# VectorE's first addition placed ahead of the first eviction in attentions 3 to 8, and a new order of PE, VectorE and ScalarE in the second attention

## The chip, the cores and the metric

One core of one Trainium2 chip. The metric is the device time of one execution in microseconds (us); the number given for a kernel is the median of several executions. The engines are TensorE (PE, with its weight loads as PEld), VectorE (DVE), ScalarE (ACT), GpSimd (POOL) and SyncE (SP), which here only issues DMAs. Each engine works through its own list of instructions in the order of the program.

## What is computed

A normalised attention for 8 batches and 12 heads, then a two-layer MLP with a tanh GELU over its output:

```python
batch, n_heads, seq, head_dim = (8, 12, 448, 64)
n_tokens, d_model, d_ff = (3584, 768, 2048)

q_n, k_n = (rmsnorm(q, g_q), rmsnorm(k, g_k))
scores = scale * np.matmul(q_n, k_n.transpose(0, 1, 3, 2))
scores = scores - np.max(scores, axis=-1, keepdims=True)
attn = np.exp(scores)
attn = attn / (np.sum(attn, axis=-1, keepdims=True) + 1e-09)
return np.matmul(attn, v).astype(np.float32)
...
h = x @ w_in
g = 0.5 * h * (1.0 + np.tanh(c * (h + 0.044715 * h * h * h)))
return (g @ w_out).astype(np.float32)
```

Inputs and output are float32; the kernel multiplies in bfloat16 and accumulates in float32.

## The kernel before

The kernel goes through the batches b = 0 to 7. Each has an attention and a first MLP layer of its own (`mm1_pair`, L516: 96 matmuls with `win`, then GELU on ScalarE). The second MLP layer of a batch (matmuls with `wout`) is spread through the attention of the next batch, so that PE has work while ScalarE computes the exponentials. The first attention (`first_attention`, L679) has another order; attentions 2 to 8 (b = 1 to 7) run in `attention` (L552), and the change touches only the two tables that it reads: `SECOND` (L545) for b = 1 and `STEADY` (L539) for b = 2 to 7, which are attentions 3 to 8.

Heads are taken four at a time: c = 0, 1, 2. For each c there are NT = 7 units t of 64 keys, so an attention has 21 units, u0 to u20. A table has three parts.

The first part is the order of PE, a string of words:

- `u`, a unit (L327): 4 matmuls give the scores of 64 keys into a two-bank PSUM buffer; ScalarE's `exp` (L341) turns it into `ex[:, t]`. Two `u` in one word follow each other directly.
- `r`, a round of the second MLP layer of the batch before (L487): 4 matmuls of 64x64 weights. 32 rounds fill one output tile in PSUM ("full"); an attention has 3 tiles, 96 rounds. `12r` is twelve rounds. In the middle of each tile, after 16 rounds, PE waits for its own last matmul (`follows`, L466).
- `s`, the sums of the exponentials for the next c (L385, weights `ones`).
- `x`, the products with V for the next c (L385, weights `vb`).

The second part is the order of VectorE:

- `A`, `B`, `F`, `G` with the number c (L353, L356, L358, L360): they add up the seven `ex[:, t]` of c, so that `s` needs fewer matmuls. `A` adds units 0, 1 and 2, 3; `B` adds 4, 5 to it; `F` folds the two halves together; `G` adds the seventh unit. For c = 2 there is no `G`. In attention 2 there is none of them for c = 1, and `s1` has 28 matmuls.
- `T`, `R`, `S`, `M` with c: transpose the sums out of PSUM (L395), reciprocal (L400), spread (L407), and `M` multiplies the product with V by it into `xT` (L420), which feeds the first MLP layer. `M` reads the PSUM buffer of `x`, `T` that of `s`.
- `E0`: evict output tile 0 from PSUM into `osb` (L505), whose stores SP issues.
- In attention 2 only: `L0`, `L1` set one element each in the buffers of raw q and k (L142), so that the loads behind them start then; `K0` is a gain on `kT` (L323), behind which GpSimd is held (L764) until it squares q and k of batch 2 (L164); `a0` to `a5` reduce these squares (L173).

The third part says before which exponential ScalarE evicts which tile: `{14: 1, 21: 2}` is tile 1 before the exponential of u14, and tile 2 after the last. In `SECOND` all three tiles are evicted by ScalarE (L511, two copies each).

The two lists are merged into one program at every word of PE: an entry of VectorE or ScalarE is put down as soon as it is at the head of its list and what it needs has been put down (`needs`, L579). This decides the order on each engine, not the times; at run time semaphores make each instruction wait for its inputs.

PSUM has four two-bank buffers in `rounds` (L66, L968). A unit, `s` or `x` takes the one that was taken longest ago (`pair`, L70):

```python
def pair(name):
    rounds.append(rounds.pop(0))
    return rounds[-1]
```

An output tile takes one out of this ring (`quartered`, L473) and puts it back at the end when it is full, so that while a tile is being filled three buffers go round. Who takes a buffer waits for the last reader of what was in it: the exponential of a unit, `T`, `M`, or the eviction of a tile.

Of the kernel before, what the change touches and what calls it, by code (L numbers as in the profile page):

```python
# [17 lines left out]
def kernel(  # L18
# [497 lines left out]
    def mm1_pair(i, cs=range(HP), b=0, js=range(2)):  # L516
# [22 lines left out]
    STEADY = (  # L539
# [4 lines left out]
    )  # L544
    SECOND = (  # L545
# [4 lines left out]
    )  # L550

    def attention(b, side, extra, ends):  # L552
# [448 lines left out]
```

## Time and profile before

| | before |
|---|---|
| median of 3 runs | 399.84 us (399.36 to 400.06) |
| the profiled execution | 400.39 us |
| its span in the profile | 398.3 us |
| granted TensorE clock | 1.00 |
| TensorE matmuls busy | 384.8 us (97%) |
| ScalarE busy | 281.6 us (71%) |
| VectorE busy | 231.5 us (58%) |
| GpSimd busy | 123.6 us (31%) |

The span is what lies between the first and the last instruction that the profile shows; the execution's own time is 2.1 us longer. In a timeline row stand the start, the duration (of all instructions merged into the row), the engine, the line of the kernel, the operation, output and input, the count, and in brackets how long the engine had been idle before it and what ended that. In the view of waits a row names who waited for whom, the sum in us, how often, and the longest. Attention 2 lies between 50.8 and 78.5 us of the span, attention 3 between 96.8 and 124.6 us, and each later one begins some 46.1 us after the one before.

### The profile page before, as it was taken

What the parts mean: (1) busy time and instruction counts of PE and PEld (TensorE: products, weight loads), DVE (VectorE), ACT (ScalarE), POOL (GpSimd) and SP (SyncE); (2) the same over time, 40 slices, a digit from 0 to 9 for tenths busy, and PEclk for the clock granted to TensorE, in tenths of its full rate; (3) what the DMA queues carried; (4) which work ended last, traced back from release to release, by engine and by line L of the source; (5) the groups of instructions that cost most, each with busy time, mean ns of one, the idle gap of its engine ahead of it and who ended that gap; (6) DMA issues with size and microseconds to landing.
All of it is one profiled execution on the core that took longest, in us unless ns stands there. A gap on an engine that the chain in (4) does not pass through costs nothing.

```text
span 398.3 us, 12138 instructions
## 1 busy us (share of the span) xinstructions
PE 384.8 (97%) x5359; PEld 231.9 (58%) x5359; DVE 231.5 (58%) x358; ACT 281.6 (71%) x361; POOL 123.6 (31%) x104
## 2 busy tenths in 40 slices
PE   8799998999999999999999999999999999999996
PEld 3365576755665566655765556655666556655564
DVE  5998837976596339925488246943499204870010
ACT  6995499777994789847995689947897359934301
POOL 4994506294008140273105440091303600000000
PEclk9999999999999999999999999999999999999999
DMA  8999999989514991359712994159622611120033
GB/s 281 306 223 207 200 187 311 195 198 254 108 44 74 268 202 46 81 135 277 135 44 51 208 238 94 43 97 267 90 53 71 131 30 41 43 63 2 0 79 81
DMA packets 66553, 54.34 MB, mean 136 GB/s; under 512 B 37572, under 2 KB 62276, under 8 KB 66500
## 3 DMA queue, kind: packets, MB, share of 16 engines
q1 hardware_dynamic: 54144, 41.48, 41.5%
q0 software_dynamic: 12128, 11.80, 19.2%
q8 instruction: 42, 0.69, 0.7%
q10 hardware_dynamic: 228, 0.28, 0.2%
q14 instruction: 11, 0.09, 0.1%
HBM read 45.61 MB, written 11.01 MB: 142 GB/s over the span
## 4 chain that ended last, share of the span: by engine, by line
PE 82%; DVE 7%; ACT 6%; DMA 2%; POOL 1%; issue 1%; SPq 0%; DVEq 0%
PE t L524 36%; PE t L487 22%; PE t L461 9%; PE t L385 9%; ACT ex L341 5%; PE t L333 5%; DVE es L356 2%; DMA rawq<-in_q_dram 2%; DVE es L353 2%; DVE osb L505 1%; DVE es L358 1%; DVE es L360 1%; POOL g L164 1%; PE h L434 1%; PE tp L294 0%
## 5 line engine op out<-in xcount | busy, mean ns | idle before, releaser
L341 ACT ACTIVATE ex<-t,shift 128x896 bf16<-128x896 f32 x168 | 155.0, 1012 | 8.0 <-PE t L333 7.0
L524 PE MATMUL t<-xT,win 128*128 128x448 bf16 x756 | 144.8, 352 | 0.0
L487 PE MATMUL t<-wout,g 64*64 64x384 bf16 x2688 | 134.7, 323 | 1.4 <-DVE xT L420 1.2
L524 PEld LDWEIGHTS <-win 128*128 128x128 bf16 x756 | 73.8, 98 | 68.9 <-issue 0.7
L531 ACT ACTIVATE g<-t 128x896 bf16<-128x896 f32 (+1 forms) x70 | 58.1, 842 | 64.6 <-PE t L524 64.6
L487 PEld LDWEIGHTS <-g 64*64 64x64 bf16 x2688 | 79.4, 107 | 36.1 <-issue 4.1
L173 DVE TENSOR_REDUCE ss<-sq 128x14 f32<-128x896 f32 (+3 forms) x45 | 44.6, 997 | 56.2 <-ACT sq L162 51.8
L333 PE MATMUL t<-qT,kT 64*64 64x448 bf16 x672 | 57.7, 351 | 2.4 <-ACT lg L198 0.9
L276 POOL TENSOR_TENSOR nrmq<-rawq,rinv 128x896 bf16<-128x896 f32 (+1 forms) x21 | 34.7, 1652 | 13.7 <-DVE o L239 6.4
L461 PE MATMUL t<-wout,g 128*128 128x384 bf16 (+1 forms) x240 | 37.6, 316 | 0.0
L764 POOL COPY mark<-es 1x1 bf16<-1x1 bf16 x6 | 1.1, 177 | 116.0 <-DVE es L358 116.0
L276 POOL TENSOR_TENSOR nrmk<-rawk,rinv 128x896 bf16<-128x896 f32 x20 | 33.6, 1679 | 0.0
L385 PE MATMUL t<-ex,vb 64*64 64x448 bf16 x588 | 31.4, 349 | 0.0
L461 PEld LDWEIGHTS <-g 128*128 128x128 bf16 x240 | 22.5, 98 | 15.0 <-issue 2.1
L395 DVE STREAM_TRANSPOSE st<-t 128x448 f32<-128x448 f32 x42 | 24.6, 623 | 9.2 <-PE t L385 9.2
L333 PEld LDWEIGHTS <-kT 64*64 64x64 bf16 x672 | 21.8, 106 | 13.0 <-DVE kT L303 2.9
L385 PEld LDWEIGHTS <-vb 64*64 64x64 bf16 x672 | 20.9, 107 | 10.8 <-issue 0.8
L407 DVE STREAM_TRANSPOSE rb<-rc 128x896 f32<-128x896 f32 (+1 forms) x25 | 26.7, 1067 | 0.3
L505 DVE COPY osb<-t 128x768 f32<-128x768 f32 x6 | 5.7, 957 | 35.9 <-PE t L487 23.2
L164 POOL TENSOR_TENSOR sq<-rawq 128x896 f32<-128x896 f32 (+1 forms) x9 | 13.6, 1511 | 36.8 <-DVE ss L173 32.7
L353 DVE TENSOR_TENSOR es<-ex 128x1792 bf16<-128x1792 bf16 x20 | 21.1, 1054 | 4.4 <-ACT ex L341 4.4
L420 DVE TENSOR_TENSOR xT<-t,rb 128x896 bf16<-128x896 f32 x21 | 22.6, 1076 | 0.9
(99 smaller groups left out, 272.5 us busy)
## 6 DMA issues: line engine op xcount, KB each, us to landing
rawq<-in_q_dram SPq DMA_DIRECT2D x23, 448.0 KB, 4.4
rawk<-in_k_dram SPq DMA_DIRECT2D x23, 448.0 KB, 5.2
out_dram<-osb SPq DMA_DIRECT2D x42, 192.0 KB, 2.7
vb<-in_v_dram POOLq DMA_DIRECT2D x6, 672.0 KB, 7.4
win<-in_moe_w_in_dram POOLq DMA_DIRECT2D x8, 384.0 KB, 10.5
wout<-in_moe_w_out_dram POOLq DMA_DIRECT2D x2, 1536.0 KB, 22.3
out_dram<-osb SPq DMA_DIRECT2D x26, 96.0 KB, 2.3
vb<-in_v_dram POOLq DMA_DIRECT2D x2, 448.0 KB, 17.8
```

What stands on the lines that cost most here:

```text
L173: nc.vector.reduce_sum(sss[b][:, seat(b, c), "qk".index(n), hs, ts], squares(b, c, n, hs, ts), axis=AX.X)
L276: eng.tensor_mul(nrms[n, b, c][:, ts].rearrange("p t a d -> p a t d"), raws[n, b, c][:, :, ts], root[:, :, ts].to_broadcast([P, 2, m, D]),)
L333: nc.tensor.matmul(sc[r * R:(r + 1) * R, a, :S], kT[rs, c, t, r], qT[b][rs, c, :, r], start=True, stop=True,)
L341: nc.scalar.activation(exs[b, c][:, t], scs.pop((b, c, t))[:, :, :S], AF.Exp, scale=scale, bias=shift)
L353: nc.vector.tensor_add(es, ex[:, :2], ex[:, 2:4])
L385: nc.tensor.matmul(o[r][a * D:(a + 1) * D], vb[b % 2][rs, 2 * c + a, i] if what else ones[rs], es[i][rs, a], start=(i == 0), stop=(i == n ...
L395: nc.vector.transpose(st[:, r].rearrange("p a b -> p (a b)"), o[r])
L407: nc.vector.transpose(oas["rb"][:, rs].rearrange("p r s -> p (r s)"), rc.to_broadcast([128, (rs.stop - rs.start) * m, 32]),)
L461: nc.tensor.matmul(o, g[:, f, i * 128:(i + 1) * 128], wout[:, f, lo:hi], start=(f == 0), stop=(f == nf - 1),)
L487: mm = nc.tensor.matmul(o[a * R:(a + 1) * R, bank, :HD], g[rs, f, at:at + R], wout[rs, f, half * HD:(half + 1) * HD], start=(turn == 0 and ...
L524: nc.tensor.matmul(h[:, j, :S], win[:, c, f * 128:(f + 1) * 128], xT[b][:, c], start=(c == 0), stop=(c == HP - 1),)
L531: nc.scalar.activation(g[:, 2 * i + ks.start:2 * i + ks.stop, (b % 2) * S:(b % 2 + 1) * S], h[:, ks, :S], AF.Gelu_apprx_tanh)
```

## The change

Two tables are replaced. In `STEADY` only the first two entries of VectorE's list change places. In `SECOND` all three parts are new.

```diff
     STEADY = (
         "2r u 2r u 12r uu 11r u 3r u 2r 3r u 4r u 4r u 5r uu 3r s 4r u 4r u 3r u 2r x 1r u 4r u 5r"
         " uu 6r su 5r u 9r u 2r xsx",
-        "E0 A0 B0 F0 G0 T0 R0 A1 S0 B1 M0 F1 G1 T1 A2 R1 B2 F2 S1 T2 M1 R2 S2 M2",
+        "A0 E0 B0 F0 G0 T0 R0 A1 S0 B1 M0 F1 G1 T1 A2 R1 B2 F2 S1 T2 M1 R2 S2 M2",
         {14: 1, 21: 2},
     )
     SECOND = (
-        "2r u 3r u 4r u 7r 1r u 7r u 3r u 5r uu 13r u 3r us 4r u 4r uu 7r u 1r xusu 2r u 7r u 1r u"
-        " 6r uu 7r x 6r s 3r x",
-        "A0 L0 B0 F0 G0 L1 T0 R0 K0 S0 a0 a1 M0 a2 T1 a3 R1 a4 S1 A2 a5 B2 F2 M1 T2 R2 S2 M2",
-        {7: 0, 14: 1, 21: 2},
+        "3r u 5r uu 8r u 7r uu 9r u 5r u 4r u 7r us 4r u 4r u 3r uu 4r x 1r usu 3r u 6r u 2r u 5r"
+        " uu 10r x 6r sx",
+        "A0 L0 B0 F0 G0 L1 T0 R0 K0 S0 a0 M0 a1 T1 a2 R1 a3 S1 A2 a4 B2 a5 F2 M1 T2 R2 S2 M2",
+        {6: 0, 14: 1, 21: 2},
     )
```

The amount of work is the same in both kernels. The lists of GpSimd and SP have the same instructions in the same order. In `SECOND` the first eviction stands before the exponential of u6 instead of u7; `M0` and `T1` each stand behind one reduction fewer (`a0` and `a1` are ahead of `M0` before, `a0` alone after), and the reductions that are left over follow later, the last between `B2` and `F2`; and with the new order of PE the ring deals out its buffers differently: before, output tile 2 takes the buffer of `x0` (which `M0` reads), after it is u15 that takes this buffer.

## The prediction

> **What bounds the kernel now.** I read the busy shares and the chain that ended last first, then the waits, then the timelines of attentions 2 and 3.
>
> ```profile
> PE 384.8 (97%) x5359; PEld 231.9 (58%) x5359; DVE 231.5 (58%) x358; ACT 281.6 (71%) x361; POOL 123.6 (31%) x104
> ...
> PE 82%; DVE 7%; ACT 6%; DMA 2%; POOL 1%; issue 1%; SPq 0%; DVEq 0%
> ```
>
> PE sets the time. The other engines enter the chain only where PE stands, so the change is worth the PE stalls that it removes or makes. The waits name them:
>
> ```profile
> ACT ex L341 <- PE t L333: 7.0, 14, 0.9
> PEld L385 <- DVE es L360: 6.0, 6, 1.0
> PE t L385 <- DVE es L360: 3.7, 6, 0.7
> PE t L487 <- DVE xT L420: 1.2, 1, 1.2
> ```
>
> Six times, once in each of attentions 3 to 8, PE waits for `G0` (L360) before `s0`. Once output tile 2 (L487) waits for `M0` (L420), in attention 2. And ScalarE waits 14 times for a unit of PE: the two engines run close together.
>
> Attention 3, in its timeline:
>
> ```profile
> 98.72 10.01 ACT L341 ACTIVATE ex<-t,shift 128x896 bf16<-128x896 f32 x11
> 103.34 0.96 DVE L505 COPY osb<-t 128x768 f32<-128x768 f32 x1 [4.62 <-PE t L487]
> 104.21 1.08 DVE L353 TENSOR_TENSOR es<-ex 128x1792 bf16<-128x1792 bf16 x1
> 105.28 0.36 PE L333 MATMUL t<-qT,kT 64*64 64x448 bf16 x4
> 105.40 1.09 DVE L356 TENSOR_TENSOR es<-es,ex 128x1792 bf16<-128x1792 bf16 x1
> 106.52 0.62 DVE L358 TENSOR_TENSOR es<-es 128x896 bf16<-128x896 bf16 x1
> 106.66 0.66 PE L487 MATMUL t<-wout,g 64*64 64x384 bf16 x12
> 107.25 0.62 DVE L360 TENSOR_TENSOR es<-es,ex 128x896 bf16<-128x896 bf16 x1
> 107.93 0.38 PE L385 MATMUL t<-es,ones 64*64 64x448 bf16 x4 [0.61 <-DVE es L360]
> 108.14 0.82 PE L487 MATMUL t<-wout,g 64*64 64x384 bf16 x16
> 108.79 0.36 PE L333 MATMUL t<-qT,kT 64*64 64x448 bf16 x4
> 108.98 0.82 PE L487 MATMUL t<-wout,g 64*64 64x384 bf16 x16
> 109.21 2.80 ACT L341 ACTIVATE ex<-t,shift 128x896 bf16<-128x896 f32 x3 [0.47 <-PE t L333]
> 111.89 0.81 ACT L505 COPY osb<-t 128x768 f32<-128x768 f32 x1
> 112.78 5.50 ACT L341 ACTIVATE ex<-t,shift 128x896 bf16<-128x896 f32 x6
> 115.69 0.36 PE L333 MATMUL t<-qT,kT 64*64 64x448 bf16 x4
> 118.31 1.09 DVE L356 TENSOR_TENSOR es<-es,ex 128x1792 bf16<-128x1792 bf16 x1
> 118.76 1.01 ACT L341 ACTIVATE ex<-t,shift 128x896 bf16<-128x896 f32 x1 [0.48 <-PE t L333]
> ```
>
> VectorE stands idle for 4.62 us until tile 0 is full, then runs E0, A0, B0, F0, G0 without a break until 107.87. Eleven exponentials take 10.01 us, one every 0.90 us and each about 1.01 long, so the fourth (u3), the last that A0 needs, ends near 98.72 + 3 x 0.90 + 1.01 = 102.43. A0 could have run in the idle time and was held by E0. A round of four L487 matmuls goes by in 0.163 us (the 16 at 108.14 until the unit at 108.79), so the three rounds from 106.66 are issued by 107.15, and `s0` stands from 107.15 to 107.93: 0.78 us, of which the profile, which counts to the modelled end of a matmul, shows 0.61.
>
> **Part 1, STEADY: A0 ahead of E0.** PE, POOL, SP and ACT keep their order; only two entries of VectorE change places. A0 starts at some 102.5, and E0 behind it at about 103.5, 0.1 to 0.2 later than before. Who waits for E0: u8, which takes tile 0's buffer (counting the ring), at 105.28. E0 ends near 104.5, so 0.8 us cover it. Tile 0's store issues with it, and nothing on PE waits for that. B0 follows at about 104.4 instead of 105.40 (its inputs u4 and u5 end at 104.23 by the same count), F0 and G0 each 1.0 earlier, and G0 is done near 106.9. PE asks for it at 107.15. The stall of 0.78 us is gone.
>
> The row for the order on VectorE is A0 at 104.21, 1.8 us after its inputs were there. The Trainium skill's page "TensorE: Matmul & The Clock Gate", section "Architectural detail: the array is 16× 32×32, not 1× 128×128", says that the scalar and vector engines keep strictly to the order of their queues. The trace agrees: A0 waited behind E0 until 103.34 + 0.87. By that rule E0 in its turn cannot pass an A0 that comes late, which is the slower rival below; without the rule the eviction would start at 103.34 as before, and the sum would be the same.
>
> What is late next is ScalarE. With PE 0.78 us ahead, u11 (108.79) is written by 108.01, its scores are there at 108.37, and ScalarE goes straight on from 108.73. So ScalarE gains only the 0.48 us from 108.73 to 109.21, and then works without a break through the eviction at 111.89 and the six exponentials from 112.78. u18 at 115.69 takes the buffer of u16, whose exponential is the third of these six: it ends at 112.78 + 2 x 0.90 + 1.01 = 115.59. That leaves 0.1 us in hand before; after, that exponential ends 0.48 earlier and u18 can't come 0.78 earlier, only some 0.5. Likewise B2 (118.31) starts when u19's exponential ends (118.28), so F2 and `s2` gain 0.5. ScalarE's second wait, 0.48 at 118.76, stays. Behind the attention come PE's own matmuls, which shift with it.
>
> I take 0.50 us for each attention, nearest to ScalarE's 0.47 of idle time. From above the bound is PE's stall, 0.78. From below I take 0.30: the chain F0, G0 or the eviction may slip by 0.1 to 0.2 where buffers come free with under 0.1 us in hand (u12, u14 and u18 by my count). Six times: 3.0 us, from 1.8 to 4.7.
>
> **Part 2, SECOND.** Attention 2, in its timeline:
>
> ```profile
> 52.38 6.61 ACT L341 ACTIVATE ex<-t,shift 128x896 bf16<-128x896 f32 x7
> 59.59 6.58 ACT L341 ACTIVATE ex<-t,shift 128x896 bf16<-128x896 f32 x7
> 59.97 0.62 DVE L360 TENSOR_TENSOR es<-es,ex 128x896 bf16<-128x896 bf16 x1
> 61.11 0.39 PE L385 MATMUL t<-es,ones 64*64 64x448 bf16 x4
> 64.66 1.52 PE L385 MATMUL t<-ex,vb 64*64 64x448 bf16 x28
> 65.33 1.09 DVE L173 TENSOR_REDUCE ss<-sq 128x14 f32<-128x896 f32 x1 [0.88 <-POOL sq L164]
> 66.03 0.89 ACT L511 COPY osb<-t 128x384 f32<-128x384 f32 x2
> 66.23 1.52 PE L385 MATMUL t<-ex,ones 64*64 64x448 bf16 x28
> 66.97 1.08 DVE L173 TENSOR_REDUCE ss<-sq 128x14 f32<-128x896 f32 x1 [0.55 <-POOL sq L164]
> 67.55 0.39 PE L333 MATMUL t<-qT,kT 64*64 64x448 bf16 x4
> 67.98 1.08 DVE L420 TENSOR_TENSOR xT<-t,rb 128x896 bf16<-128x896 f32 x1
> 69.11 0.52 PE L487 MATMUL t<-wout,g 64*64 64x384 bf16 x8 [1.18 <-DVE xT L420]
> 69.52 0.64 DVE L395 STREAM_TRANSPOSE st<-t 128x448 f32<-128x448 f32 x1
> 75.49 0.63 DVE L358 TENSOR_TENSOR es<-es 128x896 bf16<-128x896 bf16 x1
> 76.17 0.38 PE L385 MATMUL t<-es,ones 64*64 64x448 bf16 x4
> 78.49 2.82 PE L524 MATMUL t<-xT,win 128*128 128x448 bf16 x14
> ```
>
> From 52.38 to 66.03 ScalarE has fourteen exponentials and an eviction without a break, and PE, with three buffers in the ring, can't get ahead of it: until `s1` (66.23) a new order of PE gains nothing that lasts. Moving the first eviction by one exponential leaves this sum as it is. I keep u15 at 67.55.
>
> The stall behind it goes. PE was done with u15 at 67.55 + 0.19 = 67.74 (a unit goes by in 0.19: from 108.79 to the rounds at 108.98) and then stood for tile 2's buffer until M0 (67.98 + 1.08) at 69.11: 1.37 us. After, M0 stands behind a0 alone: it starts at 65.33 + 1.09 = 66.42 at the latest and ends by 67.50. Its waiter is now u15, due at 67.55, and behind it on PE everything. With `s0` ready at 60.59 + 0.06 instead of 61.11 (the old order puts it behind a unit and rounds; the new one reaches it at about 60.65), T0, R0, K0 and the squares on POOL come up to 0.46 earlier, and M0 as soon as x0 ends, so 0.05 to 0.5 us are in hand. Tile 2 now takes tile 1's buffer, free after the eviction (66.03 + 0.89 = 66.92).
>
> From 69.11 to 78.49 PE had 9.38 us of work; after has the same rounds, units, `x1`, `s2`, `x2` in another order. T1 starts behind M0 and a1 at about 68.0 (before 69.52), F2 5.97 us later before, now up to 0.6 more for one more reduction ahead of it: it ends by 68.0 + 5.97 + 0.6 + 0.63 = 75.2, and PE asks for `s2` at 67.74 + 7.49 (32 rounds of 0.163, five units of 0.19, `x1` of 1.32 like the 28 matmuls from 66.23 to 67.55) = 75.2. So 0 to 0.1 is lost there. I take 1.40 us. From below: if POOL's squares are no earlier, M0, a1 and T1 shift by 0.45, and F2 with them: 1.37 - 0.45 = 0.9. From above: 1.37 and some 0.2 because `s2` at 76.17 started right on F2's end (75.49 + 0.63 = 76.12) and may have waited for it: 1.6.
>
> **Sum.** 3.0 + 1.4 = 4.4 us, between 2.7 and 6.3. Against the profiled execution, 400.39 us (span 398.3 and 2.1 around it), that is 396.0. The median of the runs shown, 399.84, lies 0.55 lower, so I expect a median of 395.4.
>
> **The rivals.**
>
> 1. *PE's stall in attentions 3 to 8 only changes its name.* If u12, u14 or u18 wait for exponentials by all that `s0` gained, STEADY is worth nothing and 399.84 - 1.4 = 398.4 us results. For it: the 0.1 us in hand at u18. Against it: ScalarE's idle 0.47 us at 109.21, put down to PE, in the very place.
>
> 2. *All of the stall comes through.* If ScalarE makes up the missing 0.28 us in its second wait (0.48 at 118.76), it is 6 x 0.78 + 1.4 = 6.1: 393.7 us. Against it: u18 and B2 hang on exponentials that come earlier than that wait.
>
> 3. *Attention 2 gains nothing*, because u15 in place of tile 2 stands for M0, held by a0 and POOL: 399.84 - 3.0 = 396.8. Against it: M0 has one reduction fewer ahead of it, at least 1.0 us.
>
> 4. *Slower: E0 is late behind A0.* The eviction can't pass A0, and u8 stands for tile 0's buffer, with all of PE behind it. It decides if A0 starts after 103.3, since A0 and E0 take 1.9 together and u8 is due at 105.28. Were A0 released by the sixth exponential (98.72 + 5 x 0.90 + 1.01 = 104.23) in place of the fourth, E0 would end at 106.2, u8 stand for 0.9, and `s0` come 0.9 late: 6 x 0.9 = 5.4 lost, 1.4 won: 403.8 us. Against it: A0 waits for nothing but exponentials up to u3, and the idle row of 4.62 us shows VectorE free.
>
> 5. *Nothing is seen*, both parts being taken up by ScalarE: 399.8.
>
> **How the numbers follow.** Forecast 0.72 (2.7 to 6.3 off, less its ends); rival 1 0.09, rival 2 0.06, rival 3 0.05, rival 4 0.05, rival 5 0.03. The likeliest is 395.4. The bounds of both parts give 393.5 to 397.1; I end the range at 393.6, which takes in rival 2, and reach toward rival 1 on the other side: 393.6 to 397.9. About 0.2%, 0.8 us, is what a measurement can tell from no change. Faster: forecast and rivals 1 to 3, 0.92, less 0.02 for a rival 1 with a weak attention 2: 0.90. Same: 0.05. Slower: 0.05.
>
> **What would show it.** In the profile after: the wait of L385 for `es` L360 falls from 3.7 to under 0.5 us; A0 starts 3.8 us after the attention's first exponential, E0 about 1 us behind it; the exponential wait on PE (7.0) falls to about 4, one of two per attention being gone; attentions 3 to 8 follow each other by some 45.6 instead of 46.1 us; the wait of L487 for `xT` L420 is gone, and L524 starts at about 77.1 instead of 78.49. The forecast is wrong if PE waits at L333 for exponentials by more than 0.3 us in each attention, if u8 waits for L505, or if u15 of attention 2 waits for L420.

## The result, and the profile after

| | before | after |
|---|---|---|
| median, first comparison | 399.75 us (399.36 to 400.06, 4 runs) | 394.81 us (394.49 to 397.43, 4 runs) |
| ratio | | 0.9891, 95% interval 0.9848 to 0.9934 |
| median, two later comparisons | 400.47; 399.98 us | 394.29; 393.62 us |
| their ratios | | 0.9851 (0.9829 to 0.9873); 0.9834 (0.9815 to 0.9854) |
| profiled execution (first) | 400.39 us, span 398.3 | 394.85 us, span 392.7 |

The change is faster, by 4.9 us at first and by some 6 in the two later comparisons. The page of after shows PE with its share of the closing chain up from 82% to 92%, and VectorE's down from 7% to nothing:

```profile
PE 383.7 (98%) x5359; PEld 236.2 (60%) x5359; DVE 231.1 (59%) x358; ACT 280.0 (71%) x361; POOL 123.6 (31%) x104
...
PE 92%; ACT 4%; DMA 2%; POOL 1%; SPq 0%; issue 0%; DVE 0%
```

The view of waits of after has no row of L385 for L360 any more, and none of L487 for L420. ScalarE waits for units of PE half as often, and A0 is now what waits, for its exponentials, on a VectorE that has nothing else to do:

```profile
DVE es L353 <- ACT ex L341: 34.9, 7, 11.6
...
ACT ex L341 <- PE t L333: 3.5, 7, 0.8
```

Attention 3 in the timeline of after. Its first exponential starts at 98.04 (before 98.72), so 0.68 is to be taken off before's times to compare:

```profile
98.04 12.71 ACT L341 ACTIVATE ex<-t,shift 128x896 bf16<-128x896 f32 x14
101.78 1.09 DVE L353 TENSOR_TENSOR es<-ex 128x1792 bf16<-128x1792 bf16 x1 [3.79 <-ACT ex L341]
102.79 0.95 DVE L505 COPY osb<-t 128x768 f32<-128x768 f32 x1
103.65 1.08 DVE L356 TENSOR_TENSOR es<-es,ex 128x1792 bf16<-128x1792 bf16 x1
104.61 0.36 PE L333 MATMUL t<-qT,kT 64*64 64x448 bf16 x4
105.50 0.63 DVE L360 TENSOR_TENSOR es<-es,ex 128x896 bf16<-128x896 bf16 x1
106.47 0.36 PE L385 MATMUL t<-es,ones 64*64 64x448 bf16 x4
107.31 0.36 PE L333 MATMUL t<-qT,kT 64*64 64x448 bf16 x4
110.57 0.87 ACT L505 COPY osb<-t 128x768 f32<-128x768 f32 x1
110.83 0.36 PE L333 MATMUL t<-qT,kT 64*64 64x448 bf16 x4
111.30 5.53 ACT L341 ACTIVATE ex<-t,shift 128x896 bf16<-128x896 f32 x6
114.21 0.36 PE L333 MATMUL t<-qT,kT 64*64 64x448 bf16 x4
116.87 1.09 DVE L356 TENSOR_TENSOR es<-es,ex 128x1792 bf16<-128x1792 bf16 x1
117.28 1.01 ACT L341 ACTIVATE ex<-t,shift 128x896 bf16<-128x896 f32 x1 [0.44 <-PE t L333]
```

A0 starts 3.74 us behind the first exponential, E0 behind it 4.75 (before 4.62), and u8 finds tile 0's buffer free. G0 ends at 106.13, `s0` asks at 106.47 and does not wait. From there to the end everything is 0.76 to 0.80 us earlier against the first exponential: `s0` starts 8.43 behind it (before 9.21), u18 16.17 (16.97), B2 18.83 (19.59). The unit u14, at 110.83 after, stands in before's timeline as:

```profile
112.31 0.36 PE L333 MATMUL t<-qT,kT 64*64 64x448 bf16 x4
```

The chains of waits show what it is worth. The start of the same 96 matmuls in two attentions running, first of before, then of after:

```profile
124.76 18.16 PE t L524 x96
...
170.86 18.16 PE t L524 x96
```

```profile
123.29 18.16 PE t L524 x96
168.59 18.16 PE t L524 x96
```

From one attention to the next it is 46.10 us before and 45.30 after: 0.80 in each of six attentions, 4.8 us together.

Attention 2, in the timeline of after:

```profile
51.05 0.68 PE L487 MATMUL t<-wout,g 64*64 64x384 bf16 x12
66.28 1.08 DVE L420 TENSOR_TENSOR xT<-t,rb 128x896 bf16<-128x896 f32 x1
67.42 0.41 PE L333 MATMUL t<-qT,kT 64*64 64x448 bf16 x4
67.61 0.71 PE L487 MATMUL t<-wout,g 64*64 64x384 bf16 x12
68.29 0.97 PE L487 MATMUL t<-wout,g 64*64 64x384 bf16 x17
69.85 0.52 PE L487 MATMUL t<-wout,g 64*64 64x384 bf16 x7 [0.59 <-issue]
77.82 2.44 PE L524 MATMUL t<-xT,win 128*128 128x448 bf16 x12
```

And the first L487 of attention 2 in before's:

```profile
50.82 0.52 PE L487 MATMUL t<-wout,g 64*64 64x384 bf16 x8
```

M0 (66.28) is done at 67.36, u15 at 67.42 doesn't wait for it, and tile 2's first rounds follow at 67.61. But in the second group of rounds, six of four matmuls, PE breaks off after 17 of the 24 and goes on at 69.85. The 17 are issued in 0.70 us, so 0.86 are lost, and the profile names nobody ("issue"). From the first L487 to the first L524, attention 2 took 77.82 - 51.05 = 26.77 us; before it took 78.49 - 50.82 = 27.67. That is 0.90 less, not 1.40. The first attention, which the change doesn't touch, happened to end 0.23 later. 4.80 + 0.90 - 0.23 is 5.5, against 5.6 of span.

### The profile page after: what moved, and what is told of

It is laid out like the page before. It is cut to its first block, busy times and chain, and to the rows that moved or that the text cites. A ratio compares the mean times of both kernels' runs of the same rounds, so it can differ in the third digit from the quotient of the medians.

```text
span 392.7 us, 12139 instructions
## 1 busy us (share of the span) xinstructions
PE 383.7 (98%) x5359; PEld 236.2 (60%) x5359; DVE 231.1 (59%) x358; ACT 280.0 (71%) x361; POOL 123.6 (31%) x104
## 4 chain that ended last, share of the span: by engine, by line
PE 92%; ACT 4%; DMA 2%; POOL 1%; SPq 0%; issue 0%; DVE 0%
PE t L524 36%; PE t L487 28%; PE t L461 9%; PE t L385 9%; PE t L333 7%; ACT ex L341 4%; DMA rawq<-in_q_dram 2%; POOL g L164 1%; PE h L434 1%; PE tp L294 0%; PE o L385 0%; SPq L717 0%; PE os L385 0%; DVE ss L173 0%; ACT lg L198 0%
## 5 line engine op out<-in xcount | busy, mean ns | idle before, releaser
L524 PE MATMUL t<-xT,win 128*128 128x448 bf16 x756 | 144.8, 352 | 0.0
L487 PE MATMUL t<-wout,g 64*64 64x384 bf16 x2688 | 135.5, 323 | 0.6 <-issue 0.6
L524 PEld LDWEIGHTS <-win 128*128 128x128 bf16 x756 | 73.8, 98 | 68.9 <-issue 0.7
L487 PEld LDWEIGHTS <-g 64*64 64x64 bf16 x2688 | 81.8, 107 | 33.1 <-issue 3.3
L333 PE MATMUL t<-qT,kT 64*64 64x448 bf16 x672 | 58.9, 351 | 2.8 <-ACT lg L198 1.2
L333 PEld LDWEIGHTS <-kT 64*64 64x64 bf16 x672 | 24.4, 106 | 13.5 <-DVE kT L303 3.3
L385 PE MATMUL t<-ex,vb 64*64 64x448 bf16 x588 | 31.8, 349 | 0.0
L395 DVE STREAM_TRANSPOSE st<-t 128x448 f32<-128x448 f32 x42 | 24.6, 623 | 10.8 <-PE t L385 9.9
L385 PEld LDWEIGHTS <-vb 64*64 64x64 bf16 x672 | 22.6, 107 | 9.4 <-issue 0.8
L420 DVE TENSOR_TENSOR xT<-t,rb 128x896 bf16<-128x896 f32 x21 | 22.6, 1077 | 0.9
L356 DVE TENSOR_TENSOR es<-es,ex 128x1792 bf16<-128x1792 bf16 x20 | 21.5, 1077 | 0.9 <-ACT ex L341 0.9
## 6 DMA issues: line engine op xcount, KB each, us to landing
win<-in_moe_w_in_dram POOLq DMA_DIRECT2D x8, 384.0 KB, 10.6
```

What stands on the lines that cost most here:

```text
L333: nc.tensor.matmul(sc[r * R:(r + 1) * R, a, :S], kT[rs, c, t, r], qT[b][rs, c, :, r], start=True, stop=True,)
L385: nc.tensor.matmul(o[r][a * D:(a + 1) * D], vb[b % 2][rs, 2 * c + a, i] if what else ones[rs], es[i][rs, a], start=(i == 0), stop=(i == n ...
L395: nc.vector.transpose(st[:, r].rearrange("p a b -> p (a b)"), o[r])
L420: nc.vector.tensor_mul(xT[b][:, 2 * c:2 * c + 2], oas["o", c, 1][:, :, :S], oas["rb"])
L487: mm = nc.tensor.matmul(o[a * R:(a + 1) * R, bank, :HD], g[rs, f, at:at + R], wout[rs, f, half * HD:(half + 1) * HD], start=(turn == 0 and ...
L524: nc.tensor.matmul(h[:, j, :S], win[:, c, f * 128:(f + 1) * 128], xT[b][:, c], start=(c == 0), stop=(c == HP - 1),)
```

## The experiments

All times are medians beside runs of before of the same group; ratios are to these. Group one (steady_only, second_only, evict_late, loads_late) had before at 400.19 us, group two (after_again, b0_ahead, m0_late) at 400.47, group three (after_third, loads_first, loads_late_again and idle_more) at 399.98.

### Each part alone

steady_only has attention 2 as before and the rest as after:

```diff
     STEADY = (
...
-        "E0 A0 B0 F0 G0 T0 R0 A1 S0 B1 M0 F1 G1 T1 A2 R1 B2 F2 S1 T2 M1 R2 S2 M2",
+        "A0 E0 B0 F0 G0 T0 R0 A1 S0 B1 M0 F1 G1 T1 A2 R1 B2 F2 S1 T2 M1 R2 S2 M2",
```

> Attentions 3 to 8 as after, attention 2 as before. Theory: A0 ahead of E0 gives the whole of PE's stall at s0 (0.78 to 0.80 us) in each of six attentions, so 6 x 0.8 = 4.8 off: 394.95 us against a before of 399.75, and a spacing of 45.3 us between attentions. Rival (the forecast's own term): ScalarE lets only 0.50 through, the rest of the gain came from attention 2: 396.75 us.

Measured: 395.22 us, ratio 0.9874 (0.9854 to 0.9895). That is 4.97 us off, and its attentions follow each other by 45.31 us. Reordering two entries of VectorE gave all of 4.8, with attention 2 as it was: the theory holds, the forecast's own 0.50 for each attention does not.

second_only has the new table `SECOND` and the old `STEADY`.

> Attention 2 as after, attentions 3 to 8 as before. Theory: PE is rid of the 1.37 us for M0, but stands 0.75 us for its own instructions near 69.1 to 69.9, so attention 2 is 0.9 us shorter: 398.85 us against 399.75. Rival: the stall in the trace of after was a chance of that execution and the gain is the forecast 1.40: 398.35. In the profile the theory sees PE idle with 'issue' as the releaser within the six rounds behind u16.

Measured: 398.90 us, ratio 0.9974 (0.9957 to 0.9991), so 0.4 to 1.7 us off, which can't tell 0.90 from 1.40. The profile can:

```profile
50.64 0.68 PE L487 MATMUL t<-wout,g 64*64 64x384 bf16 x12
67.99 1.21 PE L487 MATMUL t<-wout,g 64*64 64x384 bf16 x24
69.27 0.38 PE L333 MATMUL t<-qT,kT 64*64 64x448 bf16 x4
76.92 3.39 PE L524 MATMUL t<-xT,win 128*128 128x448 bf16 x17
```

No break: the 24 matmuls are one row, and attention 2 took 26.28 us, 1.39 less than before. The same list of PE instructions had the break in one execution and not in another, so my theory of this run, that it belongs to the order, fell.

### The break in attention 2

Two runs moved the loads of raw q and k, on the theory that PE's instructions are brought by DMA and came late behind them. evict_late does it by way of tile 0's eviction, whose stores SP issues ahead of these loads:

```diff
-        {6: 0, 14: 1, 21: 2},
+        {7: 0, 14: 1, 21: 2},
```

> After, with the first eviction of attention 2 before the exponential of u7 again instead of u6. Theory (the loads of raw q and k behind L1 start 1.4 us earlier than before because tile 0's stores, ahead of them on SP, do, and PE's instruction fetch then queues behind them): stores and loads come about 1 us later, the fetch is in time or less late, PE's stall near 69.1 falls from 0.75 to under 0.3; u8 waits 0.2 to 0.3 for tile 0's buffer, which the pace of the exponentials hides. 0.3 to 0.6 us faster than after. Rival (the stall belongs to PE's order, not to the loads): the stall stays at 0.6 to 0.9, and the time is that of after or 0.2 longer.

loads_late, and again beside after in group three as loads_late_again:

```diff
-        "A0 L0 B0 F0 G0 L1 T0 R0 K0 S0 a0 M0 a1 T1 a2 R1 a3 S1 A2 a4 B2 a5 F2 M1 T2 R2 S2 M2",
+        "A0 L0 B0 F0 G0 T0 L1 R0 K0 S0 a0 M0 a1 T1 a2 R1 a3 S1 A2 a4 B2 a5 F2 M1 T2 R2 S2 M2",
```

> After, with the four elements of L1 set behind T0 instead of ahead of it, so that the loads of raw q and k start about 1.7 us later (near 62.8). Theory (fetch behind the loads): PE's stall near 69.1 falls under 0.3, 0.3 to 0.6 us faster than after, unless POOL's squares then wait for raw q and k by more than 1 us and hold T1 or F2. Rival (the stall belongs to PE's order): it stays at 0.6 to 0.9 in the same place, and nothing is won.

> L1 behind T0 once more, on the same chip as after. Theory: no stall after the 17 matmuls, attention 2 at 26.6 us as in the first profile (POOL's wait for raw q of 1.6 us holds F2 by some 0.3), so it is within 0.3 us of after or up to 0.3 faster: too little for a verdict, and no better kernel. Rival: what is saved at the fetch counts in full, 0.5 us faster than after.

loads_first sets L1 between B0 and F0, and with it the loads ahead of tile 0's stores on SP:

> After, with L1 ahead of F0 in attention 2, so that the loads of raw q and k go ahead of tile 0's stores on SP, near 59.4 instead of 61 us. Theory (the fetch stands behind the loads that are under way when PE asks for it, near 65 to 66 us): the loads are then done by 65.5, the fetch is in time, no stall over 0.2 us, attention 2 at 26.3 us. Rival (the earlier the loads, the later the fetch): 0.9 us of stall or more.

The changed kernel itself was run twice more:

> The changed kernel once more, beside the other three. Theory: PE's stall of 0.75 us near 69.1 in the first profile of after is not a part of the order (second_only has the same attention 2 and no such stall, 26.28 us from its first L487 to its first L524 against 26.77); this profile shows attention 2 at 26.3 us, and the time is 400.19 - 4.8 - 1.4 = 394.0 us. Rival: it comes back at the same instruction in this execution, attention 2 takes 26.8 us.

> The changed kernel a third time, as the base of this group. Theory (the block of PE's instructions that holds the 18th matmul of the six rounds behind u16 arrives late when the loads behind L1 start some 10.0 us behind attention 2's first L487, and in time when they start 10.8 us behind it or later, as in second_only, evict_late and loads_late): with the loads at 10.0 us PE stands 0.4 to 0.9 us after exactly 17 of these 24 matmuls, the third time in three profiles; attention 2 takes 26.5 to 26.8 us. Rival (chance): no stall at this place, 26.3 us.

And idle_more leaves attention 2 alone, but lengthens PE's list ahead of it, by `idle(4, warm())` in place of `idle(2, warm())` in slots 1 to 4 of the first attention. It was timed once, 395.56 us:

> After, with eight more idle matmuls on PE in the first attention (slots 1 to 4, four in place of two each), which moves everything behind them by 16 instructions in PE's list. Theory (a block of instructions that comes late): the place of the stall moves with the list, to after 9 of the 24 matmuls instead of 17, if the fetch is late in this execution; the first attention takes up to 1.5 us more. Rival (PE waits there for data): the stall stays after 17, or there is none.

What the profiles showed of attention 2, in us behind its first L487. The "fetch" is the start of the one packet of the queue of kind "instruction" ahead of the place in question, found by narrowing the window of the queues' view. The column behind it says how long after that start PE issued the matmul at the place (the 18th of the 24, in idle_more the 10th):

| run | start of the loads behind L1 | fetch | from the fetch to the matmul | lost at the break | attention 2 |
|---|---|---|---|---|---|
| after | 10.0 | 16.54 | 2.26 | 0.86, after 17 of 24 | 26.77 |
| after_again | 10.0 | 16.20 | 2.35 | 0.46, after 17 of 24 | 26.52 |
| after_third | 10.0 | 15.85 | 2.49 | none | 26.58 |
| idle_more | 10.6 | 16.73 | 2.58 | 0.68, after 9 of 24 | 27.61 |
| second_only | 10.8 | 14.44 | 3.59 | none | 26.28 |
| b0_ahead | 10.8 | 15.24 | 3.02 | none | 26.50 |
| evict_late | 11.7 | 15.94 | 2.37 | none | 26.46 |
| loads_late | 11.9 | 14.17 | 3.94 | none | 26.62 |
| loads_late_again | 12.2 | 12.88 | 5.49 | none | 26.62 |
| loads_first | 8.2 | 15.89 | 2.27 | 0.22, after 17 of 24 | 26.13 |
| m0_late (below) | 10.0 | 16.20 | 3.55 | none | 27.70 |

The small break of loads_first does not part its row, because the matmuls of a row overlap in the profile; it shows in the starts of the single matmuls, which have a gap of 0.27 us behind the 17th where 0.03 is usual.

The packet itself, in the queues' view of after for 67.5 to 68.0 us, and of second_only for 65.0 to 65.5; the columns are packets, MB and the share of 16 engines:

```profile
q1 hardware_dynamic: 113, 0.19, 100.5%
q8 instruction: 1, 0.02, 12.0%
```

```profile
q1 hardware_dynamic: 101, 0.18, 105.1%
q8 instruction: 1, 0.02, 12.1%
```

And idle_more's timeline, with all three of its breaks in attention 2:

```profile
57.93 0.35 PE L487 MATMUL t<-wout,g 64*64 64x384 bf16 x2 [0.48 <-issue]
63.85 0.68 PE L487 MATMUL t<-wout,g 64*64 64x384 bf16 x10 [0.31 <-issue]
69.11 0.65 PE L487 MATMUL t<-wout,g 64*64 64x384 bf16 x9
70.16 0.84 PE L487 MATMUL t<-wout,g 64*64 64x384 bf16 x15 [0.41 <-issue]
```

Eight more matmuls in the list moved the break from after 17 to after 9, to the matmul: it belongs to a place in PE's list of instructions, not to data. The two breaks ahead of it fit: from one of idle_more's breaks to the next PE issues 128 and 127 matmuls, and the instruction queue moves 42 packets for the 5359 matmuls of after, one for every 128. Its attention 2, 0.84 us longer than after's, has these two more.

The fetch and PE's own progress together say when there is a break. In the four runs with one, PE is ready for the matmul 1.40 to 2.05 us behind the packet's start (the table's fourth column less its fifth) and goes on 2.26 to 2.58 behind it; at idle_more's other two breaks it goes on at 2.62 and 2.60. In the seven runs without one, PE comes to the matmul 2.37 us or more behind the packet's start. m0_late shows it best: its fetch is as late as after_again's, but M0 holds PE so long that it comes to the place 3.55 us behind the fetch, and there is no break. So the wait is for a block of PE's instructions, when PE comes to it too soon behind its packet.

What makes the fetch late is not settled. The loads behind L1 start early, at 8.2 to 10.6, in all four runs with a break. But after_third had them at 10.0 too and no break, against what was expected of it; after_again had the break that its theory said was chance; and loads_first, which should have had the loads done before the fetch, still lost 0.22, a little over the 0.2 that was expected of it at most. evict_late and loads_late lost the break, as the theory said, yet were not faster for it: 394.87 us (0.9855, 0.9831 to 0.9879) and 394.12 us (0.9842, 0.9822 to 0.9863) overlap with after's three ratios, and loads_late_again came to 395.15 us (0.9868, 0.9847 to 0.9890) beside an after_third of 393.62. loads_first, 393.84 us (0.9841, 0.9820 to 0.9862), can't be told from after_third either. None of these is shown to be a better kernel than after.

One reason why so little comes of the break: u17, behind these rounds, takes the buffer of `s1` and waits for T1 anyhow. m0_late's u17 comes 0.98 us behind the start of these 24 matmuls; in second_only, which has no break, it came 1.28 behind (69.27 less 67.99), when T1 was done. In after_again, which lost 0.46, it came 1.35 behind, so 0.07 of the break counts; in after, which lost 0.86, it came 1.76 behind, so 0.48 counts. Another loss took its place in after_third:

```profile
56.94 0.33 PE L487 MATMUL t<-wout,g 64*64 64x384 bf16 x2
57.59 1.00 PE L487 MATMUL t<-wout,g 64*64 64x384 bf16 x18 [0.34 <-DMA wout<-in_moe_w_out_dram]
```

Tile 1 is the first to need the second half of `wout`, and PE stood 0.57 us (57.59 less 56.94 and two matmuls) until that had landed. The old order asked for it only at 58.13.

### M0's place

m0_late puts M0 behind a1 again, with the rest as after:

```diff
-        "A0 L0 B0 F0 G0 L1 T0 R0 K0 S0 a0 M0 a1 T1 a2 R1 a3 S1 A2 a4 B2 a5 F2 M1 T2 R2 S2 M2",
+        "A0 L0 B0 F0 G0 L1 T0 R0 K0 S0 a0 a1 M0 T1 a2 R1 a3 S1 A2 a4 B2 a5 F2 M1 T2 R2 S2 M2",
```

> After, with M0 behind a1 again in attention 2 (S0 a0 a1 M0 T1). Theory: a1 waits for POOL's second square until 66.6, M0 ends near 68.7, and u15, due at 67.4, stands 1.3 us for it, with all of PE behind it; attention 2 takes 27.6 us, as long as before, and the time is 1.3 us above after. Rival: the new order of PE by itself is what won in attention 2, and M0's place is worth under 0.4 us.

Measured: 395.57 us against 394.29 of after_again, 1.28 more. The intervals of the two ratios, 0.9851 to 0.9893 and 0.9829 to 0.9873, overlap, so it is the profile that decides: attention 2 took 27.70 us. In its timeline:

```profile
67.12 1.09 DVE L173 TENSOR_REDUCE ss<-sq 128x14 f32<-128x896 f32 x1 [0.55 <-POOL sq L164]
68.13 1.08 DVE L420 TENSOR_TENSOR xT<-t,rb 128x896 bf16<-128x896 f32 x1
69.26 0.38 PE L333 MATMUL t<-qT,kT 64*64 64x448 bf16 x4 [1.40 <-DVE rawk L142]
```

a1 waits for POOL, M0 behind it ends at 69.21, u15 starts at 69.26. The row names the tiny L142 because it is the last VectorE instruction on record then; what u15 takes is M0's buffer. So M0's place is what won in attention 2; the new order of PE alone gave nothing.

### E0 behind B0

b0_ahead is the forecast's slower rival, built:

```diff
-        "A0 E0 B0 F0 G0 T0 R0 A1 S0 B1 M0 F1 G1 T1 A2 R1 B2 F2 S1 T2 M1 R2 S2 M2",
+        "A0 B0 E0 F0 G0 T0 R0 A1 S0 B1 M0 F1 G1 T1 A2 R1 B2 F2 S1 T2 M1 R2 S2 M2",
```

> After, with E0 behind B0 as well in attentions 3 to 8 (A0 B0 E0 F0 G0). This is the forecast's slower rival, made on purpose: E0 can't pass B0, which waits for u5's exponential until some 5.6 us behind the first. E0 then ends near 7.5 us behind the first exponential, u8 asks for tile 0's buffer at 6.6. Theory: PE stands about 1.0 us at u8 in each of six attentions and nothing makes it up: 6 us slower than after, about 400. Rival: units and exponentials have room to make it up: under 2 us slower.

Measured: 400.97 us, ratio 1.0013 (0.9999 to 1.0026); 6.7 us above after_again. Its timeline:

```profile
104.14 1.09 DVE L356 TENSOR_TENSOR es<-es,ex 128x1792 bf16<-128x1792 bf16 x1 [0.72 <-ACT ex L341]
105.14 0.95 DVE L505 COPY osb<-t 128x768 f32<-128x768 f32 x1
106.15 0.38 PE L333 MATMUL t<-qT,kT 64*64 64x448 bf16 x4 [0.84 <-DVE osb L505]
106.58 5.60 ACT L341 ACTIVATE ex<-t,shift 128x896 bf16<-128x896 f32 x6 [0.68 <-PE t L333]
```

VectorE waits 0.72 us for an exponential with the eviction behind it, and u8 stands for E0. Its attentions follow each other by 46.33 us, 1.0 more than after, as expected. The position ahead of E0 that is free for A0 costs all of the gain for B0.

## Why the prediction was right, and where it was off

The time, 394.81 us, is 0.6 under the 395.4 forecast, and the direction and both mechanisms were right. The two terms of the sum were each off, in opposite ways, so that their sum came so near is in part luck: the two later comparisons have 6.2 and 6.4 us off where 4.4 were forecast.

- **A0's and E0's times** came as worked out: E0 0.13 later, B0 1.07 earlier against the first exponential, no wait at u8, G0 0.3 ahead of `s0`.
- **The step that was mis-sized is "what is late next is ScalarE", 0.50 us for each attention; it measured 0.80**, all of PE's stall, the forecast's upper bound. Rival 2 gave the right size for the wrong reason: ScalarE's second wait is still there (0.44). The room was in the first stretch. The idle 0.47 at 109.21 is counted from the end of the exponential before. But the exponentials overlap: fourteen in 12.71 us after, each 1.00 to 1.07 long, are one every 0.89 to 0.90. The eleventh started at 107.69 (98.72, ten at 0.897), so the next could have started at 108.58 and lost 0.63. A second loss left no idle row at all. Before, u14's exponential started 0.89 behind the eviction (111.89 to 112.78), because u14's scores were there only at 112.67 (112.31 and 0.36); after, it follows 0.73 behind (110.57 to 111.30), 0.16 less. 0.63 and 0.16 are the 0.8. After, this exponential still starts 0.11 behind u14's scores (110.83 and 0.36 to 111.30), as it did before: PE sets this start in both kernels, and the runs do not show how much more room ScalarE had. So the exponential that u18 waits for came 0.8 earlier as well, and u18 and B2 were no bound.
- **Attention 2, 1.40**: second_only showed 1.39, and m0_late that M0's place is its cause. In the three profiles of after it was 0.90, 1.15 and 1.09. What the sum left out is the DMA behind PE: a late block of its instructions, and the second half of `wout`, which the new order asks for earlier. In second_only u17's wait for T1, 0.3, was also missed; it was made good by u15, which came 0.24 earlier against the first L487 than before (16.49 and 16.73), so that 1.39 lies so near 1.40 is luck.
- **Rivals.** 1, 3 and 5 are out: steady_only is 4.97 us faster by itself, second_only 1.3. Rival 4's mechanism is real where the eviction stands behind an addition that is late, with the price of 1.0 us that b0_ahead shows (the forecast had 0.9); A0 is not late. The rule of the Trainium skill that was weighed there, strict order on an engine's queue ("TensorE: Matmul & The Clock Gate", "Architectural detail: the array is 16× 32×32, not 1× 128×128"), agrees with b0_ahead's row: E0 sat behind a B0 that waited 0.72 us, and u8 stood 0.84 us for E0.
- **The signs**: L385 for L360 gone, L487 for L420 gone, ScalarE's wait down to 3.5, as forecast. The spacing is 45.3, not 45.6, and L524 starts at 77.82, not 77.1 (0.23 from the first attention, 0.5 from the break).

## What to carry to other kernels

An in-order engine that is idle ahead of an instruction with a late input is the place for the next one whose inputs are there; the price to check is who waits for the instruction that now stands second, and whether the one put ahead can itself be late. When a stall goes, size the room of the next engine by the pitch of its instructions from start to start, not by the idle time that the profile prints: overlapping instructions make that too small. And a gain of a microsecond in a stretch where DMAs are busy may be shown in one profile and not in the next; run the same kernel again before naming a cause.

## What was not expected of the hardware

PE stopped in the middle of a run of matmuls that wait for nothing, 0.22 to 0.86 us, at a fixed place in its list of instructions, when it came there 1.40 to 2.05 us behind the start of a packet of the instruction queue, and went on 2.26 to 2.58 us behind it; three such places in idle_more lie 128 and 127 matmuls apart, and the profile calls the longer ones "issue". And the first attention, alike in ten of these eleven profiles and longer by eight idle matmuls in idle_more, ended anywhere from 50.26 us (evict_late) to 51.85 us (b0_ahead): a spread as large as all that attention 2 had to give, which is why the medians could not tell the variants of it apart.
